# Attention: merging the two halves of a head's output by one wide copy, a transfer and a GpSimd add

## The chip, the cores and the metric

The kernel runs on one core of a Trainium2 chip. The metric is the device time of one execution in microseconds (us); the median of three runs of the kernel before is 1149.34 us (1149.09 to 1151.95).

## The reference

The program computes an attention layer with a learned position bias, then a dense layer with three gated products, then a mixture of eight experts. Only the attention part is touched here:

```python
scores = scale * np.matmul(q, k.transpose(0, 1, 3, 2))      # B, H, S, D = 2, 8, 576, 64
scores = scores + bias.transpose(2, 0, 1)[None, :, :, :]
scores = scores - np.max(scores, axis=-1, keepdims=True)
attn = np.exp(scores)
attn = attn / (np.sum(attn, axis=-1, keepdims=True) + 1e-09)
return np.matmul(attn, v).astype(np.float32)
```

Behind it come the two expert layers, which read the attention output of all heads.

## The kernel before, in words

**Precision.** Operands of the large products are split into a high part (a rounded copy) and a low part (the value less its high part). For the values V of a head this is the job of `prep_head` (L171): GpSimd copies V into the columns `hi` of a tile `vs` (the copy goes through the helper at L66), then subtracts to make the columns `lo` (L195). The two sets of 64 columns lie side by side, so one matmul with `vs` as weights gives both products at once: 64 PSUM partitions hold the product with the high parts and 64 the product with the low parts. `pv_ev` (L546) adds these halves.

**The steps.** The attention stage is one loop over steps `s`, nine to a head; below, `k` is the step within a head and a unit `u` is a block of 128 query rows of one batch element. In step `s` the program issues, for different units, the scores (`u_qk`, TensorE, L413), the maximum with the bias (`u_max`, VectorE, L430, writes `ng`), the exponential (`u_exp`, ScalarE, L441, reads `ng`, writes `pe`), transposes of `pe` on TensorE (L492, L501), and the split of the transposed block (ScalarE makes the high part at L505, VectorE the low part at L506). The products with V of head h run at the steps of head h+1 (L543). Their results leave PSUM in `pv_ev` at k = 3, 6 and 8 of head h+1, called below the first, second and third copy: 512 columns, then 320 and 320. ScalarE copies 64 partitions of PSUM to a tile `pvt` on the other 64 partitions (L554), and VectorE adds the other half of PSUM to it and writes `x32` (L556).

**GpSimd's order.** GpSimd makes the parts of the next head: Q of batch element 0 and 1 at k = 0 and 1, K at k = 2 and 3, V at k = 6 and 8. In the odd heads 3, 5 and 7 it also runs `x_out` (L563): three passes over 576 columns for each batch element, at k = 2 and k = 4, which normalise the two finished heads and split the result. Head 7 has no next head to prepare.

**Buffers.** Tiles of the pool `up` have two buffers unless the line says otherwise: `pvt` two, `ng` three, `r` (the reciprocals of a pair of heads) one. A new tile waits until all that reads the old one in its buffer is done. The PSUM tile `pv` has one buffer.

**The SP queue.** All transfers of this stage are issued from SP in program order: the bias tile of four tiles ahead at even k, the next inputs at k = 1, and at k = 4 the reciprocals: `r_d` is written to DRAM, and two transfers `r<-r_d` bring it back, which wait for that write. A transfer that waits holds up all that stand behind it.

Of the kernel before, what the change touches and what calls it, by code (L numbers as in the profile page):

```python
# [10 lines left out]
F32 = mybir.dt.float32  # L11
# [4 lines left out]
AF = mybir.ActivationFunctionType  # L16
ALU = mybir.AluOpType
# [4 lines left out]
B, H, S, D = 2, 8, 576, 64  # L22
# [29 lines left out]
def raw(ap):  # L52
    return ap.bitcast(F32)


def make_body(stop=None):
    def body(tc, a):
        nc = tc.nc
        ctx = ExitStack()
        V, A, G, T = nc.vector, nc.scalar, nc.gpsimd, nc.tensor  # L60

        def dma(out, in_):
            nc.sync.dma_start(out=out, in_=in_)

        def pool_copy(out, in_, scale=1.0):
            G.tensor_scalar(out=out, in0=in_, scalar1=scale, scalar2=1.0, op0=ALU.mult, op1=ALU.mult)  # L66
# [4 lines left out]
        def pool(name, bufs=1, space=None, side=None):  # L71
            kw = {}
            if space is not None:
                kw["space"] = space
            if side is not None:
                kw["side"] = side
            return tc.tile_pool(name=name, bufs=bufs, **kw)

        with ctx, tc.manual_schedule():
# [91 lines left out]
            def prep_head(h, k, part=None):  # L171

                p = h % 2
                qk, vr = raw_t[h]
                if k in (0, 2):
                    b = k // 2
                    hi = qs[p][b][:, 64 * b:64 * b + S]
                    lo, src = hi[64:128], qk[:, b, 0]
                    rest, hr = src[64:128], lo
                else:  # L180
                    if k in (4, 6):
                        b = k // 2 - 2
                        hi, lo, src = kh[p][b], kl[p][b], qk[:, b, 1]
                    else:
                        b = k - 7
                        oh = 64 * (h % 2)
                        ol = 64 - oh
                        hi, lo, src = vs[p][b][:, :, oh:oh + D], vs[p][b][:, :, ol:ol + D], vr[:, b]
                    rest, hr = src, hi
                if part in (None, 0):  # L190
                    pool_copy(hi, src)
                n = lo.shape[1]
                m = (n + 1) // 2
                for sl in {None: (slice(0, n),), 0: (), 1: (slice(0, m),), 2: (slice(m, n),)}[part]:
                    G.tensor_tensor(out=lo[:, sl], in0=rest[:, sl], in1=raw(hr[:, sl]), op=ALU.subtract)  # L195
# [12 lines left out]
            with ExitStack() as bctx:  # L208
# [80 lines left out]
                for q in range(2):  # L289
                    V.tensor_tensor(  # L290
                        out=wf[:, q, :].rearrange("p (i h) -> p i h", h=H),
                        in0=ab[:, q, :].unsqueeze(1).to_broadcast([128, 4, H]),
                        in1=msk.rearrange("p (i h) -> p i h", h=H), op=ALU.mult)
# [45 lines left out]
                v3 = lambda x: x.rearrange("p (f n) -> p f n", f=3)  # L339
# [14 lines left out]
                for g16 in range(NG16):  # L354
                    ps = bias_mm(g16)
# [31 lines left out]
            with ExitStack() as actx:  # L387
                pt_p = actx.enter_context(pool("pt"))
                up = actx.enter_context(pool("up", bufs=2))
# [6 lines left out]
                CW = (256, 320)  # L396
# [25 lines left out]
                def u_max(u):  # L422
                    h, k = divmod(u, 9)
                    w = un[u]
                    ng = up.tile([128, S], F32, tag="ng", name="ng", bufs=3)
                    if k == 0:

                        st_t[h] = up.tile([128, 2, 9], F32, tag="st", name="st", bufs=3)
                    c = U_COL[k]
                    V.tensor_tensor_reduce(  # L430
                        out=ng.rearrange("p (f n) -> p f n", f=2), in0=w["sc"][:, :, :SH],
                        in1=bias_t[h, k // 2].rearrange("p (f n) -> p f n", f=2),
                        op0=ALU.add, op1=ALU.min, scale=-0.125, scalar=3.0e38, accum_out=st_t[h][:, 0, c:c + 1])
                    w["ng"] = ng
# [94 lines left out]

                x32 = [None]  # L530
                pvs = {}

                def pv_mm(h, ch, bs, i0, i1):
                    if i0 == 0:
# [11 lines left out]
                def pv_ev(h, ch, bs):  # L546
                    ps = pvs.pop((h, ch, bs))
                    om = 64 * (h % 2)
                    oc = 64 - om
                    if h % 2 == 0 and ch == 0:  # L550
                        x32[0] = up.tile([128, 2, S], F32, tag="x32", name="x32")
                    n = len(bs) * CW[ch]
                    tmp = up.tile([128, 512], F32, tag="pvt", name="pvt")
                    A.activation(out=tmp[om:om + 64, :n], in_=ps[oc:oc + 64, :n], func=AF.Copy)  # L554
                    v3 = lambda x: x.rearrange("p (b i) -> p b i", b=len(bs))
                    V.tensor_tensor(out=x32[0][om:om + 64, bs[0]:bs[-1] + 1, 256 * ch:256 * ch + CW[ch]],  # L556
                                    in0=v3(ps[om:om + 64, :n]), in1=v3(tmp[om:om + 64, :n]), op=ALU.add)
                    if h % 2 == 1 and ch == 0:
                        x_t[h] = x32[0], r_t[0]

# [26 lines left out]
                def m1_first(n):  # L587

                    for _ in range(n):
# [9 lines left out]
                PV = {0: (9, 0, (0, 1), 0, 6), 1: (10, 0, (0, 1), 6, 12), 2: (11, 0, (0, 1), 12, 18),  # L599
                      4: (13, 1, (0,), 0, 5), 5: (14, 1, (0,), 5, 9), 7: (16, 1, (1,), 0, 9)}  # L600
                EV = {3: (12, 0, (0, 1)), 6: (15, 1, (0,)), 8: (17, 1, (1,))}
                PREP = {0: 0, 1: 2, 2: 4, 3: 6, 6: 7, 8: 8}
                LAGL = (5, 4, 3, 3, 4, 3, 3, 3, 4)
                R = {2: (11, r_add, r_inv), 3: (12, r_tr), 4: (13, r_out)}

                def at(f, u):
                    if 0 <= u < NU:
                        return f(u)

                for s in range(NU + 18):  # L610
                    h, k = divmod(s, 9)
                    at(u_qk, s)
                    if s == 1:
                        pv = ps_v.tile([128, 512], F32, tag="pv", name="pv")
                        for _ in range(NW2):
                            T.matmul(out=pv, lhsT=qs[0][0][:, 0:128], rhs=qs[0][0][:, 0:512], start=True, stop=True)
                    at(u_tr, s - 3)
                    for d in (5, 4, 3):
                        if s >= d and LAGL[(s - d) % 9] == d:
                            at(u_trl, s - d)  # L620
                    at(u_max, s - 1)
                    lo = at(u_ev, s - 4)
                    at(u_exp, s - 2)
                    if lo is not None:
                        lo()
                    if k in R and 0 <= (s - R[k][0]) // 9 < H:
                        for f in R[k][1:]:
                            f((s - R[k][0]) // 9)
                    if s < NU and k in PREP and h + 1 < H:
                        prep_head(h + 1, PREP[k])  # L630
                    for off, b in ((20, 0), (22, 1)):
                        if s > off and (s - off) % 18 == 9 and (s - off) // 9 < H - 1:
                            x_out((s - off) // 9, b)
                    if k in EV and 0 <= (s - EV[k][0]) // 9 < H:
                        pv_ev((s - EV[k][0]) // 9, *EV[k][1:])
                    for d, e in ((4, 3), (4, 7), (5, 8)):
                        lo = at(u_evl, s - d) if (s - d) % 9 == e else None
                        if lo is not None:
                            lo()
                    if k in PV and 0 <= (s - PV[k][0]) // 9 < H:  # L640
                        pv_mm((s - PV[k][0]) // 9, *PV[k][1:])
                    if k in W_AT and s < NU:
                        w_step(last=2)
                    elif s >= NU + 4:
                        w_step(2, last=3)
                    if s < NU:
                        if k % 2 == 0 and 5 * h + k // 2 + 4 < 5 * H:
                            load_bias(5 * h + k // 2 + 4)
                        if k == 1:
                            load_head(h + 2)  # L650
                    un.pop(s - 6, None)
                    if s == NU + 2:
                        for b in range(B):
                            x = x32[0][:64, b]
                            G.tensor_tensor(out=x, in0=x, in1=r_t[0][:64, b], op=ALU.mult)
                    if s == NU + 4:
                        r_mm()
                    m1_first(EARLY.get(s, 0))
                    if s - 9 * (H - 1) in (15, 17):
                        x_last((s - 9 * (H - 1) - 15) // 2)  # L660
# [18 lines left out]
            with ExitStack() as mctx:  # L679
# [8 lines left out]
                with pool("mp", bufs=2) as mp:  # L688
                    w_pool[:] = mp, 6
                    for f in range(6):  # L690
                        for g in range(NTG):
# [3 lines left out]
                            t2 = mp.tile([128, TG], F32, tag="t2", name="t2")  # L695
# [105 lines left out]
                for n, g in enumerate((0, 2, 1, 3)):  # L801
# [3 lines left out]
                    for d in range(4):  # L805
                        p = ps_o.tile([128, 512], F32, tag="o", name="o")
                        k = 0
# [294 lines left out]
```

## Time and profile before

| | us |
|---|---|
| median of three runs | 1149.34 |
| the profiled execution, its time | 1150.27 |
| the profiled execution, its span | 1148.5 |
| attention stage, from the first L430 to the last L578 | about 83 to 232 |

The profile shows one execution. Times in its rows are counted from the span's start. Engines are PE (TensorE; PEld its weight loads), DVE (VectorE), ACT (ScalarE), POOL (GpSimd); SPq is SP's queue of transfers. Over the whole span PE is busy 97%, DVE 62%, ACT 44% and POOL 33%.

### The profile page before, as it was taken

Reading aid. Unit: us, or ns where it says so; the run is one execution under the profiler, and the core shown is the slowest. Engines: PE = TensorE matmul, PEld = TensorE weight load, DVE = VectorE, ACT = ScalarE, POOL = GpSimd, SP = SyncE. Lnnn points to the kernel's source line nnn. Section 1 sums busy time; section 2 is a strip of 40 time slices with the busy share of each in tenths; the row PEclk is TensorE's granted clock in tenths of the full one; section 3 lists DMA queues with packets and bytes.
Section 4 is the critical chain, followed back from the end, with each engine's and each line's share of the span. In section 5 each row is a group of like instructions: output and inputs, shape, how many; then the busy total and the mean of one; then the engine's idle time right before and its main releaser. Section 6 shows DMA issues by size and latency. Waiting matters only on the chain.

```text
span 1148.5 us, 18982 instructions
## 1 busy us (share of the span) xinstructions
PE 1115.9 (97%) x7578; PEld 999.8 (87%) x7578; DVE 711.9 (62%) x1241; ACT 506.7 (44%) x879; POOL 373.3 (33%) x307
## 2 busy tenths in 40 slices
PE   6989999999999999999999999999999999999998
PEld 3448889999999899898998989989899898998986
DVE  7999999787752766554645636446365463554633
ACT  5988988633333553341522505325143151341520
POOL 3996789222212613220311202113022131220310
PEclk8999999999999999999999999999999999999999
DMA  3666665123310210210201102112021120210102
GB/s 140 229 230 216 210 187 166 41 92 110 111 42 14 93 37 13 62 47 28 74 26 49 49 27 74 37 38 70 14 65 40 34 74 10 64 47 28 56 19 82
DMA packets 35286, 87.45 MB, mean 76 GB/s; under 512 B 5439, under 2 KB 5630, under 8 KB 34302
## 3 DMA queue, kind: packets, MB, share of 16 engines
q1 hardware_dynamic: 35054, 85.96, 23.5%
q8 instruction: 59, 0.97, 0.3%
q10 hardware_dynamic: 144, 0.29, 0.1%
q14 instruction: 29, 0.24, 0.1%
HBM read 73.23 MB, written 13.01 MB: 75 GB/s over the span
## 4 chain that ended last, share of the span: by engine, by line
PE 70%; DVE 16%; issue 4%; ACT 2%; DMA 1%; DVEq 0%; ACTq 0%; SPq 0%
PE d L1014 34%; PE x L932 11%; PE y L932 8%; PE z L932 8%; PE o L810 3%; DVE ng L430 3%; DVE ptl L506 3%; PE m L584 2%; DVE ww L105 1%; DVE ww L108 1%; DVE ww L110 1%; DVE pth L506 1%; DVE x L556 1%; DMA wf<-in_moe_w 1%; ACT ww L104 1%
## 5 line engine op out<-in xcount | busy, mean ns | idle before, releaser
L1025 DVE SCALAR_TENSOR_TENSOR acc<-d,P,acc 128x512 f32<-128x512 f32 x135 | 101.3, 750 | 240.1 <-PE d L1014 240.0
L1000 POOL TENSOR_TENSOR w2l<-w2r,w2h 128x512 fp32r<-128x512 f32 x64 | 94.0, 1470 | 465.3 <-ACT w2h L999 457.0
L1014 PE MATMUL d<-w2h,hh 128*128 128x512 f32 x576 | 225.0, 391 | 0.0
L1014 PE MATMUL d<-w2h,hl 128*128 128x512 f32 x576 | 224.7, 390 | 0.0
L1014 PE MATMUL d<-w2l,hh 128*128 128x512 f32 x576 | 224.3, 389 | 0.0
L940 ACT ACTIVATE s<-x 128x576 f32<-128x576 f32 x96 | 62.5, 651 | 355.3 <-PE x L932 352.1
L945 ACT ACTIVATE hh<-s 128x576 fp32r<-128x576 f32 x128 | 87.9, 687 | 95.6 <-DVE s L957 46.3
L1014 PEld LDWEIGHTS d<-w2h,hl 128*128 128x128 f32 x576 | 108.1, 188 | 23.1 <-DVE hl L950 0.3
L1014 PEld LDWEIGHTS d<-w2l,hh 128*128 128x128 f32 x576 | 108.2, 188 | 22.1
L1014 PEld LDWEIGHTS d<-w2h,hh 128*128 128x128 f32 x576 | 108.2, 188 | 21.8
L950 DVE SCALAR_TENSOR_TENSOR hl<-s,hh 128x576 fp32r<-128x576 f32 x128 | 103.4, 826 | 1.7 <-ACT hh L945 1.5
L750 POOL TENSOR_TENSOR w1l<-wf,w1h 128x768 fp32r<-128x768 f32 x32 | 59.3, 1853 | 76.6 <-ACT w1h L749 76.6
L932 PE MATMUL x<-xth,w1h 128*128 128x288 f32 x384 | 82.6, 297 | 0.5 <-ACT acc L813 0.5
L932 PE MATMUL x<-xtl,w1h 128*128 128x288 f32 x384 | 82.2, 296 | 0.0
L932 PE MATMUL x<-xth,w1l 128*128 128x288 f32 x384 | 82.1, 295 | 0.0
L584 PE MATMUL m<-xh,wh 128*128 128x384 f32 x216 | 74.1, 343 | 1.8 <-DVE t L702 1.8
L333 PE MATMUL p<-s,wb 128*32 128x192 f16 (+1 forms) x1152 | 60.9, 295 | 13.1 <-DVE s L307 8.0
L584 PE MATMUL m<-xl,wh 128*128 128x384 f32 x216 | 73.6, 341 | 0.0
L584 PE MATMUL m<-xh,wl 128*128 128x384 f32 x216 | 73.5, 340 | 0.0
L333 PEld LDWEIGHTS <-wb 128*32 128x32 f16 x1152 | 31.8, 97 | 42.4 <-issue 31.1
L966 DVE TENSOR_TENSOR s<-y,s 128x576 f32<-128x576 f32 x32 | 24.2, 758 | 70.8 <-ACT w1h L753 58.9
L932 PEld LDWEIGHTS x<-xth,w1h 128*128 128x128 f32 x384 | 62.5, 188 | 2.0 <-ACT acc L813 0.7
(186 smaller groups left out, 2547.1 us busy)
## 6 DMA issues: line engine op xcount, KB each, us to landing
wf<-in_moe_w SPq DMA_DIRECT2D x32, 512.0 KB, 3.5
w2r<-in_moe_w SPq DMA_DIRECT2D x64, 256.0 KB, 2.6
bias_d<-bo SPq DMA_DIRECT2D x36, 288.0 KB, 2.7
bias<-bias_d SPq DMA_DIRECT2D x32, 288.0 KB, 3.6
wr<-in_moe_w SPq DMA_DIRECT2D x18, 512.0 KB, 3.7
qk<-in_qk SPq DMA_DIRECT2D x7, 1152.0 KB, 6.9
wr<-in_moe_w_out SPq DMA_DIRECT2D x6, 512.0 KB, 3.6
vr<-in_v SPq DMA_DIRECT2D x8, 320.0 KB, 4.3
```

What stands on the lines that cost most here:

```text
L333: T.matmul(out=thirds(pt)[32 * c:32 * c + 32, sl, :], lhsT=wb[p][:, q, :], rhs=s_t[4 * g16 + c][:, sl, :], start=(p == 0), stop=(p == 1))
L430: V.tensor_tensor_reduce(out=ng.rearrange("p (f n) -> p f n", f=2), in0=w["sc"][:, :, :SH], in1=bias_t[h, k // 2].rearrange("p (f n) -> p ...
L506: return lambda: V.tensor_tensor(out=lo, in0=src, in1=raw(hi), op=ALU.subtract)
L584: T.matmul(out=p[:, :TG], lhsT=ws[:, 128 * c:128 * c + 128], rhs=xs[:, c, TG * g:TG * g + TG], start=(c == 0 and n == 0), stop=(c == 3 and ...
L750: G.tensor_tensor(out=lo[:, 0:3], in0=t[:, 1:4], in1=raw(hi[:, 0:3]), op=ALU.subtract)
L932: T.matmul(out=ps[bank][:, s, :SH], lhsT=ws[:, i, c, :], rhs=xs[:, j, c, s * SH:s * SH + SH], start=(start and k == 0), stop=(k == 5), **kw)
L940: A.activation(out=t, in_=src, func=AF.Copy)
L945: A.activation(out=o, in_=src, func=AF.Relu)
L950: V.scalar_tensor_tensor(out=l, in0=src, scalar=0.0, in1=raw(o), op0=ALU.max, op1=ALU.subtract)
L1000: G.tensor_tensor(out=lo, in0=r, in1=raw(hi), op=ALU.subtract)
L1014: T.matmul(out=pd, lhsT=hs[:, fh, 128 * t:128 * t + 128], rhs=ws, start=(k == 0), stop=(k == 11))
L1025: V.scalar_tensor_tensor(out=acc[:, t, :], in0=pd, scalar=P[:, t, e:e + 1], in1=acc[:, t, :], op0=ALU.mult, op1=ALU.add)
```

## The change

- The high part of V for the next head (k = 6 and 8) is a copy on ScalarE and no longer on GpSimd. The low part stays on GpSimd.
- `pv_ev` for heads 0 to 6: ScalarE copies all 128 partitions of PSUM into `pvt`; a transfer from the SP queue moves the 64 partitions of the other half into a new tile `pv2` with one buffer; GpSimd adds the two halves into `x32`. The add is put off: it is issued two steps after the copy, that is at k = 5, 8 and 1 (of the next head), before `x_out` of the same step and behind `prep_head`. Head 7 keeps the old way.
- `ng` has two buffers in place of three.

```diff
-                if part in (None, 0):
+                if part is None and k > 6:
+                    A.activation(out=hi, in_=src, func=AF.Copy)
+                elif part in (None, 0):
                     pool_copy(hi, src)
...
-                    ng = up.tile([128, S], F32, tag="ng", name="ng", bufs=3)
+                    ng = up.tile([128, S], F32, tag="ng", name="ng", bufs=2)
...
+                adds = []
...
                     tmp = up.tile([128, 512], F32, tag="pvt", name="pvt")
-                    A.activation(out=tmp[om:om + 64, :n], in_=ps[oc:oc + 64, :n], func=AF.Copy)
...
+                    if h < H - 1:
+
+                        t2 = up.tile([128, 512], F32, tag="pv2", name="pv2", bufs=1)
+                        A.activation(out=tmp[:, :n], in_=ps[:, :n], func=AF.Copy)
+                        dma(t2[om:om + 64, :n], tmp[oc:oc + 64, :n])
+                        adds.append((9 * h + PV_AT[ch, bs] + 2, lambda: G.tensor_tensor(
+                            out=out, in0=v3(tmp[om:om + 64, :n]), in1=v3(t2[om:om + 64, :n]), op=ALU.add)))
+                    else:
+                        A.activation(out=tmp[om:om + 64, :n], in_=ps[oc:oc + 64, :n], func=AF.Copy)
+                        V.tensor_tensor(out=out, in0=v3(ps[om:om + 64, :n]), in1=v3(tmp[om:om + 64, :n]), op=ALU.add)
...
+                PV_AT = {e[1:]: e[0] for e in EV.values()}
...
+                    while adds and adds[0][0] <= s:
+                        adds.pop(0)[1]()
```

## Rows read from the trace of the kernel before

**Rows 1.** Windows by head, third copy to third copy: length, then busy time per engine

```profile
core 0: us, PE busy (x) PEld busy (x) DVE busy (x) ACT busy (x) POOL busy (x), PEclk, DMA share, GB/s
110.35:127.39 17.04, 16.54 (x127) 15.42 (x125) 16.67 (x37) 15.33 (x36) 11.58 (x13) 1.00 0.53 177
127.39:143.98 16.59, 16.02 (x125) 15.15 (x124) 16.30 (x36) 15.31 (x35) 15.83 (x15) 1.00 0.70 230
143.98:161.61 17.63, 16.05 (x120) 14.48 (x119) 17.31 (x37) 15.22 (x34) 14.52 (x17) 1.00 0.62 200
161.61:178.74 17.13, 16.32 (x124) 15.03 (x123) 16.84 (x38) 14.96 (x35) 16.24 (x15) 1.00 0.56 180
178.74:195.45 16.71, 16.55 (x129) 15.67 (x128) 16.33 (x37) 15.05 (x35) 15.39 (x18) 1.00 0.51 130
195.45:211.42 15.97, 15.83 (x125) 15.19 (x124) 15.69 (x36) 14.56 (x34) 9.26 (x8) 1.00 0.39 122
110.35:211.42 101.07, 97.32 (x737) 90.95 (x736) 99.15 (x216) 90.43 (x207) 82.82 (x83) 1.00 0.55 174
```

**Rows 2.** Chain that ended last, 110.35 to 211.42 us, shares by line

```profile
by line: DVE ng L430 29.0%; DVE ptl L506 24.9%; issue 11.4%; DVE pth L506 8.6%; DVE x L556 7.2%; PE sc L413 4.5%; PE pv L543 3.6%; DVE st L448 3.2%; PE pt L492 2.4%; DVE st L430 1.5%; DVE ww L106 0.7%; DVE ww L110 0.7%; DVE ww L108 0.7%; AC
```

**Rows 3.** Groups by form, 110.35 to 211.42 us: count, busy us, mean ns, idle before

```profile
L556 DVE TENSOR_TENSOR x<-pv,pvt 64x320 f32<-64x320 f32 x12 | 5.8, 484 | 0.2
L556 DVE TENSOR_TENSOR x<-pv,pvt 64x512 f32<-64x512 f32 x6 | 4.1, 684 | 0.1
...
L554 ACT ACTIVATE pvt<-pv 64x320 f32<-64x320 f32 x12 | 5.2, 433 | 0.3
L554 ACT ACTIVATE pvt<-pv 64x512 f32<-64x512 f32 x6 | 3.6, 592 | 0.1
L505 ACT ACTIVATE pth<-pt 128x512 fp32r<-128x512 f32 x54 | 32.1, 595 | 8.7 <-PE pt L492 7.7
...
L66 POOL TENSOR_SCALAR vs<-vr 128x320 fp32r<-128x320 f32 x11 | 5.4, 492 | 9.6 <-PE pv L543 9.6
L195 POOL TENSOR_TENSOR vs<-vr,vs 128x320 fp32r<-128x320 f32 x11 | 9.9, 903 | 0.9
L113 POOL TENSOR_TENSOR wl<-ww,wh 128x512 fp32r<-128x512 f32 x2 | 2.6, 1291 | 0.1
L568 POOL TENSOR_TENSOR x<-x,r 128x576 f32<-128x576 f32 x6 | 8.6, 1431 | 0.0
```

**Rows 4.** Timeline, ACT at 182 and DVE at 183 us: an exponential, the next-but-one maximum

```profile
182.43 0.77 ACT L441 ACTIVATE pe<-ng,st 128x576 f32<-128x576 f32 x1
...
183.19 0.74 DVE L430 CUSTOM_DVE_ANT_0 ng<-sc,bias 128x576 f32<-128x576 f32 x1
```

**Rows 5.** Timeline of POOL: the stretches up to the end of x_out, heads 3 and 5

```profile
128.23 0.68 POOL L66 TENSOR_SCALAR qs<-qk 128x576 fp32r<-128x576 f32 x1
...
145.63 0.46 POOL L66 TENSOR_SCALAR vs<-vr 128x320 fp32r<-128x320 f32 x1
...
162.94 0.68 POOL L66 TENSOR_SCALAR qs<-qk 128x576 fp32r<-128x576 f32 x1
...
180.17 0.46 POOL L66 TENSOR_SCALAR vs<-vr 128x320 fp32r<-128x320 f32 x1
```

**Rows 6.** Timeline of ACT: the third copy of head 3

```profile
143.98 0.43 ACT L554 ACTIVATE pvt<-pv 64x320 f32<-64x320 f32 x1
```

**Rows 7.** Timeline of SP's queue: the reciprocals of two heads coming back

```profile
125.97 1.26 SPq L63 DMA_DIRECT2D r<-r_d  x2
...
159.22 1.26 SPq L63 DMA_DIRECT2D r<-r_d  x2
```

**Rows 8.** DMA issues, 96 to 212 us: KB each, median us to landing

```profile
bias<-bias_d SPq DMA_DIRECT2D x14, 144.0 KB, 3.0
```

**Rows 9.** Windows as in rows 1, where the granted clock was low

```profile
224.00:226.00 2.00, 2.00 (x8) 2.00 (x8) 1.28 (x3) 0.53 (x2) 0.00 (x0) 0.50 0.00 0
226.00:228.00 2.00, 2.00 (x12) 2.00 (x11) 1.20 (x3) 1.22 (x2) 1.29 (x1) 0.79 0.51 152
```

More of the change, by code (lines that the diff above doesn't have):

```diff
@@ L553, in pv_ev @@
                     tmp = up.tile([128, 512], F32, tag="pvt", name="pvt")
-                    A.activation(out=tmp[om:om + 64, :n], in_=ps[oc:oc + 64, :n], func=AF.Copy)
                     v3 = lambda x: x.rearrange("p (b i) -> p b i", b=len(bs))
-                    V.tensor_tensor(out=x32[0][om:om + 64, bs[0]:bs[-1] + 1, 256 * ch:256 * ch + CW[ch]],
-                                    in0=v3(ps[om:om + 64, :n]), in1=v3(tmp[om:om + 64, :n]), op=ALU.add)
+                    out = x32[0][om:om + 64, bs[0]:bs[-1] + 1, 256 * ch:256 * ch + CW[ch]]
+                    if h < H - 1:
[7 more added lines that the diff above has]
+                        V.tensor_tensor(out=out, in0=v3(ps[om:om + 64, :n]), in1=v3(tmp[om:om + 64, :n]), op=ALU.add)
                     if h % 2 == 1 and ch == 0:
```

## The prediction

> **What bounds the kernel now.** I looked first at the windows by head, because the change touches the attention stage alone and the shares of the whole span say nothing of it. From the third copy of head 1 at 110.35 us to that of head 7 at 211.42 us six heads take 101.07 us; DVE is busy 99.15 of them, 98%, PE 97.32, ACT 90.43 and POOL 82.82 [rows 1]. The reader should see that one engine is full and that the other three are not far behind. Then the chain that ended last: it runs along DVE's maximum, its low parts and the adds of L556, which alone hold 7.2% [rows 2]. So DVE sets the pace, and work taken off DVE can shorten a head, until the next engine is full. Third, the waits beside the groups: POOL idles 9.6 us for PE ahead of the copies of V [rows 3]. That looks like room for adds, but it must be seen head by head: POOL is busy 15.83 of 16.59 us and 16.24 of 17.13 us in the stretches that hold the x_out passes of heads 3 and 5, and 9.26 of 15.97 us in the last [rows 1]. Its room is where head 7 prepares nothing and where no x_out runs.
>
> **Part 1: DVE is relieved.** Per head one add of 0.684 and two of 0.484 us go [rows 3], 1.65 us; DVE's 99.15 / 6 = 16.5 us become 14.9. ACT gains two copies of V of 320 columns; the nearest row is the copy of 64x320, 0.433 us [rows 3], so 0.87 us: 90.43 / 6 = 15.07 becomes 15.9 us. The PSUM copy over 128 partitions instead of 64 costs nothing more: 128x512 took 595 ns and 64x512 592 ns [rows 3]. At k = 6 and 8 the new copies wait for the same matmuls as the PSUM copy right behind them, so they add no wait. PE's weight loads are busy 90.95 / 6 = 15.2 us [rows 1]. An undisturbed head would then take 16.1 us, just above ACT's sum; at best 15.2 (PE), at worst 16.4. Against rows 1 this saves 0.9 us in the stretch 110.35:127.39, 1.5 in 143.98:161.61, 0.6 in 178.74:195.45, nothing in 195.45:211.42, and I give 0.5 to head 1, where two of the three adds fall before its third copy. **Saving 3.5 us**; with 15.2 us a head 1.8 + 2.4 + 1.5 + 0.8 and 1.0 for head 1, 7.5; with 16.4 us 0.6 + 1.2 + 0.3 + 0.2, 2.3. The stretches of heads 3 and 5 are not in this sum: part 3 has them.
>
> **Part 2: two buffers for ng.** A maximum then waits for the exponential of two units before. In the tightest place I found that exponential ends at 182.43 + 0.77 = 183.20 us and the maximum starts at 183.19 [rows 4]; elsewhere there is more. I take 0: with DVE relieved and PE feeding it, DVE has no reason to be earlier. Cover gone, 0.5 us in all.
>
> **Part 3: POOL is late in heads 3 and 5, and ACT has to wait for it.** This decides. pvt has two buffers, so the third copy (k = 8) takes the buffer of the first copy (k = 3) and must wait until the add of that one has been made on POOL. That add is issued at k = 5, behind everything POOL has before it: Q and K of the next head, the add of the previous head's third copy, and both x_out passes. Before the change DVE freed that buffer within the step.
>
> The prices: an add of 512 columns between 1.29 us (two inputs, 512 columns, L113) and 1.43 us (576, L568); an add of 320 columns 0.90 us (L195) [rows 3]. I take 1.36 and 0.89.
>
> Head 3: POOL starts it at 128.23 us and works without a gap until both x_out passes are done at 145.63, 17.40 us [rows 5]. Now two adds stand in between, 2.25 us: 19.65. The start moves too. At the least the add of head 2's second copy comes in at k = 8 and one copy of V goes (0.89 us less 0.49 and its spacing, 0.35 us). At the most that add waits for its transfer, which sits in SP's queue behind the reciprocals that are issued at 125.97 for 1.26 us [rows 7]: one more bias issue of some 0.35 us, then 3.0 us for a transfer of 144 KB, the nearest in size to 80 KB [rows 8], so landing near 130.6, add done 131.5. The add of the first copy ends between 128.58 + 19.65 = 148.2 and 131.5 + 19.65 = 151.15 us. The third copy of head 3 ran at 143.98 [rows 6]. The stretch grows by 4.2 to 7.2 us; I take 5.5. In those clocks all parts shift alike by what heads 1 and 2 gain, so this holds whatever they gain.
>
> The Trainium skill ("DMA: Bandwidth & Descriptors", the section on fixed cost) puts some 2.0 us fixed on a transfer plus its bytes at 436 GB/s. By that an 80 KB transfer would be an estimated 2.2 us and the upper end 0.8 us lower; 80 KB within the core was not measured here.
>
> Head 5: POOL works from 162.94 to 180.17, 17.23 us [rows 5], and with two adds 19.5. Start at the least 0.35 later, at the most behind the reciprocals at 159.22 [rows 7]: 159.22 + 1.26 + 0.35 + 3.0 + 0.89 = 164.7. The add ends at 182.8 to 184.2, against a third copy at 178.74 [rows 1]: 4.1 to 5.5 us, I take 4.7. Head 7's third copy is safe, since POOL prepares nothing there.
>
> What stands behind ACT's wait: the high part of the next transposed block, without which DVE cannot make its low part, and the exponentials, without which PE has nothing to transpose. There are two score buffers and two ng buffers, so PE and DVE run ahead by about a step and then stand too; I let them win back 0.5 us after each wait (0 to 1). **Cost 5.5 + 4.7 - 1.0 = 9.2 us**, between 6.3 and 12.7.
>
> SP: three issues more per head, about 0.35 us each, and the transfer waits for ACT's copy and for pv2, which the previous add frees. Behind it stand the bias loads; they are issued four tiles ahead and while ACT waits nobody asks for them. I cost this at nothing; if that cover goes it is a late bias of 1 to 2 us in head 6.
>
> **The sum.** 9.2 - 3.5 = +5.7 us on the profiled execution: 1150.27 + 5.7 = 1156.0. Its time lies 0.93 us above the median of the runs, so on that scale 1149.34 + 5.7 = **1155.0 us**. The ends of the terms: 6.3 - 7.5 = -1.2 and 12.7 + 0.5 - 2.3 = +10.9, so 1148 to 1160.
>
> **The rivals.**
> *A, POOL keeps up and the relief of DVE counts in every head.* For it: 9.6 us of POOL's idle time [rows 3], and the adds are put off by two steps. Against: that idle time is not in front of the late adds. Heads 3 and 5 would also go to 16.1 us: 3.5 + 0.5 + 1.0 = 5.0 us saved, 1144.3. It decides if the add at k = 5 ends before the third copy in heads 3 and 5, that is if POOL's stretch there is under about 16 us. Chance 0.13.
> *B, the wait is there but costs about what is saved.* The wait at its low end, 8.3 less 2.0 won back, against savings of 6 to 7: within 1 us of 1149.3. Chance 0.17.
> *C, the pauses also cost clock.* At 224 to 226 us the granted clock was 0.50, the 1.2 GHz level, and 0.79 in the next 2 us, after a row of small matmuls [rows 9]: at 0.50 two us are worth one, so 1.0 + 0.4 = 1.4 us lost there. If PE standing for 4 us twice brought that each time, 2.8 us more: 1157.8. The Trainium skill ("TensorE: Matmul & The Clock Gate", Part 1) says an idle array falls back to 1.2 GHz; no row of this stage has such a pause, so no trace here shows it. Chance 0.20.
> The forecast itself 0.50.
>
> **How the numbers follow.** About 0.3%, 3.4 us, is what can be told from no change. The forecast and C lie above +3.4 us, with a tail of the forecast below: slower 0.68, same 0.19, faster 0.13. The range takes the upper end of the sum with C, cut at 1161, and reaches below into B, 1147.5; it leaves out A and the top of C.
>
> **What would show it.** Right: in the waits, ACT at the copy of heads 3 and 5 standing 4 to 7 us for POOL; third copies of heads 3 and 5 some 21 to 22 us after those of heads 2 and 4; other heads near 16.1; no L556 before head 7; POOL without idle time in heads 3 and 5. Wrong: no ACT wait on POOL over 2 us (then A), undisturbed heads still near 17 (then part 1 is too large), a granted clock under 1.00 between 140 and 200 us (then C).

## The result

The changed kernel takes 1161.43 us in the median of four runs (1159.2 to 1164.12), the kernel before 1149.68 beside it: a ratio of 1.0101, with a 95% interval of 1.0088 to 1.0115. It is slower, and by 11.8 us where 5.7 were forecast. The profiled execution took 1162.18 us with a span of 1160.4, 11.9 more than the span before, and that is what the profile has to account for.

The windows by head of the changed kernel, from third copy to third copy as in [rows 1] (columns as there):

```profile
109.30:126.66 17.36, 16.98 (x137) 16.54 (x136) 16.39 (x37) 15.42 (x39) 12.16 (x12) 1.00 0.63 196
126.66:152.95 26.29, 17.32 (x128) 15.35 (x125) 14.29 (x34) 15.17 (x37) 21.11 (x21) 0.95 0.54 172
152.95:168.92 15.97, 15.48 (x109) 15.09 (x110) 13.79 (x32) 14.62 (x37) 13.25 (x14) 0.88 0.64 203
168.92:192.18 23.26, 17.49 (x138) 16.59 (x136) 16.46 (x39) 14.79 (x38) 20.25 (x20) 0.98 0.55 168
192.18:208.62 16.44, 15.95 (x109) 15.88 (x110) 13.53 (x30) 15.09 (x37) 15.04 (x15) 0.83 0.52 138
208.62:225.17 16.55, 16.53 (x134) 16.02 (x132) 15.29 (x37) 14.18 (x35) 10.94 (x11) 1.00 0.41 127
109.30:225.17 115.87, 99.75 (x746) 95.47 (x744) 89.74 (x202) 89.27 (x218) 92.75 (x89) 0.94 0.55 168
```

The six stretches take 115.87 us instead of 101.07. DVE is busy 89.74 us instead of 99.15, so the relief is there; but no engine is full any more, and the time is idle time. Two stretches hold the loss, those that end at the third copies of heads 3 and 5: 26.29 instead of 16.59 and 23.26 instead of 17.13, together 15.83 us more.

The chain through the same time, against [rows 2]: DVE's maximum and its adds are gone from the front, and POOL, the new transfer and PE stand there.

```profile
by line: PE pv L546 10.7%; DMA pv<-pvt 10.6%; PE sc L415 9.3%; POOL x L564 8.8%; POOL x L579 7.3%; PE pt L494 7.2%; issue 6.9%; POOL xl L581 6.2%; POOL qs L197 4.9%; POOL kl L197 4.1%; ACT pe L443 3.7%; POOL xh L66 3.5%; DVE ptl L508 2.7%; 
```

The longest waits from 90 to 235 us (who waited for whom: us in total, times, longest). The copy out of PSUM is L562 now, the add L564, the maximum L432:

```profile
DVE ptl L508 <- ACT pth L507: 23.5, 13, 8.8
ACT pvt L562 <- POOL x L564: 21.5, 6, 9.1
...
PE pv L546 <- ACT pvt L562: 15.9, 4, 8.2
POOL x L564 <- DMA pv<-pvt: 14.3, 7, 4.3
```

Read from the bottom: POOL waits for the transfer, ACT for POOL's add, PE and DVE for ACT. The longest ACT waits are the third copies of heads 3 and 5; ACT's timeline shows them:

```profile
126.66 0.44 ACT L562 ACTIVATE pvt<-pv 128x320 f32<-128x320 f32 x1 [1.08 <-POOL x L564]
...
152.95 0.44 ACT L562 ACTIVATE pvt<-pv 128x320 f32<-128x320 f32 x1 [9.07 <-POOL x L564]
...
192.18 0.44 ACT L562 ACTIVATE pvt<-pv 128x320 f32<-128x320 f32 x1 [7.65 <-POOL x L564]
```

POOL's timeline around them, to be read beside [rows 5]: the adds of head 2's first and second copy, POOL's first work for head 3, the add of head 3's first copy; then, from the add of the second copy on, the same for heads 4 and 5.

```profile
125.34 1.28 POOL L564 TENSOR_TENSOR x<-pvt,pv 64x512 f32<-64x512 f32 x1 [2.60 <-ACT pe L443]
...
132.63 0.86 POOL L564 TENSOR_TENSOR x<-pvt,pv 64x320 f32<-64x320 f32 x1 [4.21 <-PE pt L494]
133.58 0.67 POOL L66 TENSOR_SCALAR qs<-qk 128x576 fp32r<-128x576 f32 x1
...
151.67 1.25 POOL L564 TENSOR_TENSOR x<-pvt,pv 64x512 f32<-64x512 f32 x1
...
172.63 0.88 POOL L564 TENSOR_TENSOR x<-pvt,pv 64x320 f32<-64x320 f32 x1 [2.07 <-PE pl L503]
173.60 0.68 POOL L66 TENSOR_SCALAR qs<-qk 128x576 fp32r<-128x576 f32 x1
...
190.89 1.25 POOL L564 TENSOR_TENSOR x<-pvt,pv 64x512 f32<-64x512 f32 x1
```

POOL starts head 3 at 133.58 us, 6.92 after the third copy of head 2; before it was 128.23, 0.84 after. From there it works 151.67 + 1.25 - 133.58 = 19.34 us to the end of the add of the first copy, and the third copy starts 0.03 us later. POOL starts head 5 4.68 us after the third copy of head 4 (1.33 before), and its work there takes 18.54 us. The profile names PE as what released the late adds; an add reads nothing of PE's, and what it needs besides ACT's copy is the transfer. SP's queue shows that transfer (it is named pv<-pvt):

```profile
119.36 0.50 SPq L63 DMA_DIRECT2D r_d<-rt  x1
124.86 1.26 SPq L63 DMA_DIRECT2D r<-r_d  x2
126.22 0.54 SPq L63 DMA_DIRECT2D bias<-bias_d  x1
126.93 0.49 SPq L63 DMA_DIRECT2D pv<-pvt  x1
...
133.52 0.49 SPq L63 DMA_DIRECT2D pv<-pvt  x1
```

The second copy was made at 121.83 us. Its transfer stands behind the reciprocals, which wait until 124.86 for their own write, and goes out at 126.93. The reciprocals were not all that held it: pv2's one buffer was in use until the add of the first copy was done, at 125.34 + 1.28 = 126.62. The transfer then lands 5.6 us after its issue, and the add starts 5.7 us after it. The third copy's transfer waits for pv2's buffer in turn, until 133.52.

Last, the granted clock around the first pause and behind the second (windows, columns as in [rows 9]), and two scores matmuls on PE's timeline at either level:

```profile
148.00:150.00 2.00, 0.00 (x0) 0.00 (x0) 0.00 (x0) 0.00 (x0) 1.91 (x3) 1.00 0.00 0
150.00:152.00 2.00, 0.00 (x0) 0.00 (x0) 0.00 (x0) 0.00 (x0) 1.92 (x3) 0.52 0.43 126
152.00:154.00 2.00, 0.56 (x2) 0.56 (x3) 0.09 (x1) 1.05 (x3) 2.00 (x3) 0.50 0.62 169
...
192.00:196.00 4.00, 3.33 (x16) 3.28 (x16) 2.50 (x5) 3.44 (x8) 3.44 (x6) 0.50 0.58 163
```
```profile
154.89 0.44 PE L415 MATMUL sc<-kh,qs 128*128 128x288 f32 x1
155.13 0.44 PE L415 MATMUL sc<-kl,qs 128*128 128x288 f32 x1
...
157.62 0.29 PE L415 MATMUL sc<-kh,qs 128*128 128x288 f32 x1
157.76 0.29 PE L415 MATMUL sc<-kl,qs 128*128 128x288 f32 x1
```

While PE, DVE and ACT all stand and only POOL works, the granted clock falls to 0.50, the 1.2 GHz level, and PE restarts at 0.24 us a matmul instead of 0.14. The stretch after each long pause has a mean clock of 0.88 and 0.83. "TensorE: Matmul & The Clock Gate" of the Trainium skill (Part 1) says that an idle array falls back to 1.2 GHz; in these two pauses the trace agrees.

### The profile page after: what moved, and what is told of

Its sections match the earlier page's. It is cut to its first block, busy times and chain, and to the rows that moved or that the text cites. A ratio compares the mean times of both kernels' runs of the same rounds, so it can differ in the third digit from the quotient of the medians.

```text
span 1160.4 us, 19007 instructions
## 1 busy us (share of the span) xinstructions
PE 1115.7 (96%) x7578; PEld 999.7 (86%) x7578; DVE 700.8 (60%) x1220; ACT 506.6 (44%) x893; POOL 384.7 (33%) x314
## 4 chain that ended last, share of the span: by engine, by line
PE 71%; DVE 8%; POOL 4%; ACT 3%; issue 3%; DMA 2%; SPq 0%; POOLq 0%; DVEq 0%; ACTq 0%
PE d L1028 34%; PE x L946 12%; PE y L946 8%; PE z L946 8%; PE o L824 3%; PE m L595 2%; PE sc L415 1%; PE pv L546 1%; DMA pv<-pvt 1%; DVE ww L105 1%; DVE ww L110 1%; DVE ww L108 1%; POOL x L564 1%; PE pt L494 1%; POOL x L579 1%
```

## The experiments

The theory after the result: POOL is late in heads 3 and 5, by the length of its own work and by transfers that come late, and ACT pays because pvt has two buffers. The rivals put the loss down to one of the parts: the buffers, the transfers, POOL's work, SP's order, or the two small edits. Each ratio is to the kernel before on the same chip, with its 95% interval. Four runs pay for a buffer with the fifth buffer of pe; a run with four buffers of pe and nothing else was not made, but in the waits of these four no exponential waits for a buffer of pe.

**Three buffers for pvt.** The space comes from pe, four buffers instead of five.

```diff
-                    pe = up.tile([128, S], F32, tag="pe", name="pe", bufs=5)
+                    pe = up.tile([128, S], F32, tag="pe", name="pe", bufs=4)
...
-                    tmp = up.tile([128, 512], F32, tag="pvt", name="pvt")
+                    tmp = up.tile([128, 512], F32, tag="pvt", name="pvt", bufs=3)
```

> The changed kernel with three buffers for pvt (paid for by four instead of five for pe). Theory (ACT's waits for the add on POOL, through the two buffers of pvt, make the loss): the third copies of heads 3 and 5, which waited 9.1 and 7.7 us, wait under 1 us; these heads go from 26.3 and 23.3 us to 16.5 to 17.5, the granted clock stays at 1.00, and the time falls by 12 to 15 us to 1146 to 1149. Rival (POOL has too much work in heads 3 and 5, and any buffer only moves the wait on): ACT's wait goes, but PE or SP waits for POOL instead, heads 3 and 5 stay above 20 us, and the time falls by less than 6 us, to 1156 or more.

Measured: 1157.99 us, ratio 1.0062 (1.0045 to 1.0079). The theory as I had put it fell. The rival held in the time and in the waits, but not in the heads it named: head 3 takes 17.3 us, and the loss moves on to heads 4, 5 and 6 with 21.7, 22.1 and 20.5 us. The wait at the third copies is gone; the waits from 143 to 200 us show where it went:

```profile
ACT pth L507 <- PE pt L494: 10.7, 10, 4.5
DVE ng L432 <- DMA bias<-bias_d: 7.7, 5, 2.3
...
POOL x L564 <- DMA pv<-pvt: 6.2, 4, 3.5
...
PEld sc L415 <- POOL kh L66: 2.6, 1, 2.6
PEld sc L415 <- POOL kl L197: 2.5, 3, 1.3
```

PE waits for K of the next head and DVE for a bias that is late: the reciprocals in front of it in SP's queue wait for their own write and for the passes of x_out that read their one buffer, which POOL makes late. The buffer of pvt is where POOL's lateness is felt first, and not the only place.

**No transfer.** The copied half is added to itself, so the other half is left out of the sum.

```diff
-                        t2 = up.tile([128, 512], F32, tag="pv2", name="pv2", bufs=1)
...
-                        dma(t2[om:om + 64, :n], tmp[oc:oc + 64, :n])
...
-                            out=out, in0=v3(tmp[om:om + 64, :n]), in1=v3(t2[om:om + 64, :n]), op=ALU.add)))
+                            out=out, in0=v3(tmp[om:om + 64, :n]), in1=v3(tmp[om:om + 64, :n]), op=ALU.add)))
```

> The changed kernel without the transfers: GpSimd adds the copied half to itself, so the other half is left out of the sum. Theory (POOL starts heads 3 and 5 late because the transfer of the second copy lands late, behind the reciprocals in SP's queue, and adds to a wait that is there anyway): POOL's first instruction for head 3 comes at most 2 us after the third copy of head 2 instead of 6.9, that of head 5 at most 2 instead of 4.7; ACT's waits fall from 9.1 and 7.7 to 3 to 5 us each; the time falls by 7 to 10 us to 1151 to 1154. Rival (the length of the adds alone): the waits fall by less than 1.5 us each and the time by less than 4 us.

Measured: 1153.21 us, ratio 1.0022 (1.0013 to 1.0032), 8.2 us below the changed kernel. POOL starts heads 3 and 5 1.94 us after the third copy in both, and ACT still waits, as its timeline shows:

```profile
148.26 0.44 ACT L561 ACTIVATE pvt<-pv 128x320 f32<-128x320 f32 x1 [5.19 <-POOL x L562]
...
185.12 0.44 ACT L561 ACTIVATE pvt<-pv 128x320 f32<-128x320 f32 x1 [2.85 <-POOL x L562]
```

Both waits lie a little outside the 3 to 5 us expected. So the late transfers are the larger part of the loss, and a wait remains without them. The 8.2 us are an upper bound for them, since these adds, which read one tile twice, are also shorter: 0.72 us for 320 columns against 0.87.

**The V copies alone** (the first edit of the diff on the kernel before).

> The kernel before with the high part of V on ScalarE and nothing else changed. Theory (ACT has room while DVE sets the pace): within 1 us of the kernel before, 1149 to 1150.5. Rival (the copies hold up ACT's exponentials at k = 6 and 8): 2 to 6 us slower, 1152 to 1156.

Measured: 1150.01 us, ratio 0.9998 (0.9989 to 1.0008). By themselves they cost and bring nothing that is clear of the noise.

**Two buffers for ng alone** (the second edit on the kernel before).

> The kernel before with two buffers for ng and nothing else changed. Theory (the exponential is done by the time the maximum two units later starts): 0 to 0.5 us slower, 1149.5 to 1150.2. Rival (DVE, which sets the pace, now waits for ACT every few units): 3 us slower or more, 1152.5 and up.

Measured: 1150.24 us, ratio 0.9994 (0.9985 to 1.0004). Nothing clear of the noise either.

**The reciprocals later.** The two transfers r<-r_d move out of `r_out` into a function of their own, three steps later.

```diff
+                def r_back(h):
...
-                R = {2: (11, r_add, r_inv), 3: (12, r_tr), 4: (13, r_out)}
+                R = {2: (11, r_add, r_inv), 3: (12, r_tr), 4: (13, r_out), 7: (16, r_back)}
```

> The changed kernel with the reciprocals' two transfers issued at k = 7 instead of k = 4, so that the transfer of the second copy (k = 6) no longer stands behind them in SP's queue. Theory (that place in the queue makes POOL start heads 3 and 5 late): the transfer of head 2's second copy is issued within 2 us of its copy instead of 5.1, POOL's first instruction for head 3 comes at most 3 us after the third copy of head 2 instead of 6.9; ACT's waits at the third copies of heads 3 and 5 fall to 5 to 7 and 3.5 to 5.5 us; the time falls to 1153.5 to 1157. Rival (the transfers are late by themselves, by their own landing time and by pv2's one buffer): POOL still starts head 3 over 4.5 us after the third copy, and the time stays above 1158.5.

Measured: 1155.71 us, ratio 1.0056 (1.0040 to 1.0072), 5.7 us below the changed kernel. ACT waits 6.89 and 5.20 us, and POOL starts head 3 3.06 us after the third copy, a hair outside what was expected. One expectation missed: the second copy's transfer goes out 4.3 us after its copy and not within 2, because it now waits for pv2, whose add waits for its own transfer. The rows show the transfer, its add, and then the stretches of heads 3, 5 and 6 (windows, columns as in [rows 1]):

```profile
127.55 0.48 SPq L63 DMA_DIRECT2D pv<-pvt  x1
...
129.65 0.87 POOL L568 TENSOR_TENSOR x<-pvt,pv 64x320 f32<-64x320 f32 x1 [0.33 <-DMA pv<-pvt]
...
127.55:150.06 22.51, 16.76 (x132) 15.86 (x130) 15.47 (x34) 15.29 (x37) 21.20 (x21) 0.99 0.58 183
...
166.79:188.23 21.44, 18.07 (x142) 17.12 (x140) 17.29 (x39) 14.99 (x38) 20.20 (x20) 1.00 0.55 168
188.23:203.45 15.22, 14.13 (x109) 13.51 (x110) 13.05 (x30) 14.89 (x37) 14.15 (x14) 1.00 0.63 173
```

The transfer goes out together with the third copy (127.55), hardly sooner than in the changed kernel (0.27 us after it). What changed in head 3 is the time from its issue to its add: 2.1 us, where it was 5.7 with the reciprocals issued just ahead of it. In head 5 both changed: it goes out 0.77 us before the third copy instead of 0.46 after, and the add follows 2.1 us later instead of 3.25. Why a transfer lands later behind the reciprocals, no run shows.

**Two buffers for pv2** (four for pe).

```diff
-name="pv2", bufs=1)
+name="pv2", bufs=2)
```

> The changed kernel with two buffers for pv2 (paid for by four instead of five for pe) and nothing else. Theory (pv2's one buffer and the place behind the reciprocals each make the transfers late; the place is the larger part): the transfer of head 2's second copy still goes behind the reciprocals, that of the third copy no longer waits for an add; POOL starts head 3 4 to 6.5 us after the third copy of head 2; the time is 1157 to 1161. Rival (pv2's buffer is the whole delay): POOL starts head 3 at most 3 us after the third copy, time 1153 to 1156.

Measured: 1157.64 us, ratio 1.0065 (1.0047 to 1.0082). POOL starts head 3 4.4 us after the third copy. The buffer brings 3.8 us, the place in the queue 5.7.

**Both.**

> The changed kernel with two buffers for pv2 (four for pe) and the reciprocals' transfers at k = 7: both causes of the late start are gone, the two buffers of pvt stay. Theory (what is left is the length of POOL's own work before the add of the first copy, 19.5 us against some 16 to the third copy): POOL starts heads 3 and 5 at most 3 us after the third copy before them, ACT waits 4.5 to 6.5 us in head 3 and 3.5 to 5.5 in head 5, time 1152.5 to 1156. Rival (the waits were made by the late transfers): ACT's waits under 2.5 us each, time under 1150.

Measured: 1155.29 us, ratio 1.0041 (1.0026 to 1.0056), 6.1 us below the changed kernel and not clear of the run with the later reciprocals alone: the two gains do not add up. POOL starts heads 3 and 5 2.8 and 2.1 us after the third copy, and ACT still waits:

```profile
150.66 0.44 ACT L566 ACTIVATE pvt<-pv 128x320 f32<-128x320 f32 x1 [6.90 <-POOL x L568]
...
187.50 0.44 ACT L566 ACTIVATE pvt<-pv 128x320 f32<-128x320 f32 x1 [5.20 <-POOL x L568]
```

The first wait is 0.4 us over what I expected, the second inside. With more punctual transfers the change still loses 4.7 us on the kernel before (1155.29 less 1150.6): this is what the longer work of POOL costs and the relief of DVE does not pay back, with whatever the clock adds.

**Three buffers for pvt and the reciprocals later.**

> The changed kernel for all heads, with three buffers for pvt (four for pe) and the reciprocals' transfers at k = 7: neither the buffer nor the place in the queue holds anybody up. Theory (POOL's own work, about 21 us in heads 3 and 5 and 13.7 in heads 2, 4 and 6, is then the bound, 17.4 us a head over a pair): heads 3 and 5 above 17.5 us and the time at 1150 to 1154. Rival (the two waits were all): heads 3 and 5 at 16.5 us, time 1145 to 1148.

Measured: 1151.41 us, ratio 1.0014 (1.0004 to 1.0025). No copy waits over 0.8 us for an add now. The stretches that end at the third copies of heads 5 and 6 (windows, columns as in [rows 1]):

```profile
160.11:179.90 19.79, 16.49 (x125) 15.18 (x125) 16.43 (x35) 15.11 (x37) 15.00 (x15) 1.00 0.71 221
179.90:199.36 19.46, 17.23 (x127) 15.47 (x126) 14.51 (x32) 15.55 (x38) 18.19 (x19) 1.00 0.44 121
```

Head 3 is not held up (16.30 us), against what I expected; heads 5 and 6 pay, 19.79 and 19.46 us. That POOL's work is the bound is not shown: it is busy 18.19 us of the second stretch, but only 15.00 of the first, where it stands 3.8 us for a transfer, that of a copy made at 150.21 us, which waited for pv2's one buffer until 158.57 and landed 7.9 us later, while DVE waits 2.9 us for a bias. So late transfers still have a part in it.

**Only heads 1, 3 and 5 the new way**, so that no first or second copy of an x_out head goes over POOL.

```diff
-                    if h < H - 1:
+                    if h % 2 and h < H - 1:
```

> The changed kernel with the new way only for heads 1, 3 and 5, whose copies fall in steps of the even heads 2, 4 and 6, where POOL runs no x_out; all other heads keep the copy of 64 partitions and the add on VectorE. Theory (the loss is in heads 3 and 5 alone, the relief of DVE pays elsewhere): no wait of ACT for POOL over 1 us, heads 2, 4 and 6 at 16.0 to 16.6 us, heads 3 and 5 at 16.5 to 17.5, time 1146 to 1149.5. Rival (POOL still starts the odd heads 5 us or more late, and bias or K come late): heads 3 and 5 above 18 us, time 1151 to 1155.

Measured: 1152.03 us, ratio 1.0022 (1.0011 to 1.0033): the rival, though in another head than it said. Heads 3 and 5 take 16.28 and 17.43 us, but head 4 takes 21.0: POOL starts head 3 5.2 us after the third copy, with the transfer still behind the reciprocals; x_out then frees the reciprocals' one buffer late, SP sends them at 148.49 us instead of 143.42, and from 143 to 165 us DVE waits 2.0 us for a bias and PE 1.7 for K.

**The same with the reciprocals later.**

> Both: the new way only for heads 1, 3 and 5, and the reciprocals' transfers at k = 7. Theory: as in the run with heads 1, 3 and 5 alone, and POOL starts heads 3 and 5 at most 3 us after the third copy before them; time 1145.5 to 1148.5. Rival (DVE is not relieved where it matters, or ACT's copies of V cost as much): within 1 us of the kernel before, 1149.5 to 1151.5.

Measured: 1146.93 us, ratio 0.9974 (0.9964 to 0.9983). This beats both kernels. Its windows by head:

```profile
111.22:127.88 16.66, 16.17 (x127) 15.40 (x126) 15.73 (x37) 15.53 (x38) 10.88 (x11) 1.00 0.65 206
127.88:144.16 16.28, 16.09 (x126) 15.37 (x125) 15.37 (x37) 15.75 (x38) 15.19 (x16) 1.00 0.75 245
144.16:161.58 17.42, 16.82 (x133) 16.10 (x132) 16.73 (x38) 15.19 (x37) 16.43 (x15) 1.00 0.65 197
161.58:178.11 16.53, 14.72 (x109) 13.20 (x108) 15.35 (x32) 15.59 (x37) 15.38 (x15) 1.00 0.67 210
178.11:194.00 15.89, 15.89 (x129) 15.69 (x129) 14.96 (x36) 15.23 (x38) 15.10 (x15) 1.00 0.56 154
194.00:209.00 15.00, 15.00 (x121) 14.65 (x120) 14.39 (x33) 14.45 (x35) 11.74 (x11) 1.00 0.43 111
```

97.78 us in place of 101.07, 3.3 less, with a clock of 1.00 in every head. POOL is at work 16.43 of 17.42 us in the fullest stretch, and one copy there still waits 1.24 us for it. Where the gain comes from is not shown: 1.4 us of it fall in heads 2, 4 and 6, whose adds left DVE, and 1.9 in heads 3, 5 and 7, which keep theirs. The three small edits together (V on ScalarE, two buffers for ng, reciprocals later) without any add moved were not run.

**The control: the reciprocals later, on the kernel before.**

> The kernel before with the reciprocals' two transfers at k = 7 and nothing else changed: the control for the run that was faster than both kernels. Theory (that run gained by the relief of DVE; the transfers' place matters only to the new transfers): within 0.8 us of the kernel before, 1149 to 1150.7. Rival (the gain came from the place in the queue): 2 to 3.5 us faster than the kernel before.

Measured: 1149.53 us, ratio 0.9994 (0.9985 to 1.0003). That is 1.1 us below the kernel before beside it, a little more than expected but not clear of the noise. So the faster run did not gain by the queue's order alone.

**All heads but 2, 4 and 7 the new way, reciprocals later.**

```diff
-                    if h < H - 1:
+                    if h not in (2, 4) and h < H - 1:
```

> The new way for all heads but 2, 4 and 7, with the reciprocals' transfers at k = 7: heads 0 and 6, whose copies fall in steps of heads 1 and 7, are added to heads 1, 3 and 5; only the copies in steps of heads 3 and 5 stay the old way. Theory (every head in which POOL has room gains by DVE's relief): head 1 and head 7 each 0.3 to 0.8 us shorter than with heads 1, 3 and 5 alone, time 1145.5 to 1147. Rival (these heads are held by PE and ACT by now): the same as with heads 1, 3 and 5, 1146.5 to 1148.

Measured: 1147.43 us, ratio 0.9973 (0.9962 to 0.9983), the same as with heads 1, 3 and 5. The rival held: heads 0 and 6 bring nothing more that could be told.

## Why the prediction was right and wrong

**Right: the sign, the place and the mechanism.** ACT stands at the third copies of heads 3 and 5 for POOL's add of the first, with DVE and PE behind it.

**Right: the length of POOL's work.** 19.34 and 18.54 us against 19.65 and 19.5; the adds took 0.87 and 1.27 us against 0.89 and 1.36. With the reciprocals later and nothing else changed the loss is 5.8 us (1155.71 less 1149.87), where 5.7 were forecast, and there the terms fit too: heads 3 and 5 take 10.2 us more than before (forecast 10.2), the stretches of heads 2, 4, 6 and 7 together 4.6 less (forecast 3.0, and 1.0 won back). The sum I made was that of a kernel whose transfers land sooner. That the totals agree to 0.1 us is luck: that profile also holds 1.2 us lost up to the third copy of head 1 and 2.3 gained after that of head 7, which no term forecast.

**Wrong: when POOL starts.** The step that failed is "then 3.0 us for a transfer of 144 KB, the nearest in size to 80 KB, so landing near 130.6, add done 131.5", which I had called the most. The transfer was issued when the sum said, 0.27 us after the third copy of head 2 (the sum: 127.58 against 127.39), but it landed 5.6 us later and not 3.0. Landing took 2.6 us in the median for 80 KB and 4.6 for 128 KB, and from 2.0 to 5.6 over those 12 of the 21 transfers whose landing the profile tells:

```profile
pv<-pvt SPq DMA_DIRECT2D x14, 80.0 KB, 2.6
...
pv<-pvt SPq DMA_DIRECT2D x7, 128.0 KB, 4.6
```

A median of another transfer is no upper bound. "DMA: Bandwidth & Descriptors" of the Trainium skill (the section on the anatomy of one DMA, whose fit is for transfers issued from GpSimd) led to an estimate of 2.2 us for 80 KB; issued from SP, the quick ones here took 2.0 and the late one 5.6. The start came 6.92 and 4.68 us after the third copies, where the sum allowed 4.1 and 3.1 at most, and the values I took, 5.5 and 4.7 us of growth, stand for about 2.4 each. In head 3 the landing is 2.6 of the 2.8 us above the most. In head 5 it was 3.1 us, as assumed; there the reciprocals went out 0.8 us later against the third copy than before, and the bias and the transfer behind them 0.5 later than costed. Starts later by 4.5 and 2.3 us than taken, with work shorter by 0.3 and 1.0, make 10.2 + 6.8 - 1.3 = 15.7 us, where the two stretches grew by 15.83. Of the changed kernel's 11.8 us some 5.7 go with the place of the reciprocals in SP's queue, which is what moving them takes away. I had seen that order, and still cost SP "at nothing"; the issues, too, took 0.49 us each and not 0.35.

**Wrong: only two waits.** Four other copies waited too: 1.08 us for the third of head 2, 0.99 and 1.06 for the first and second of head 3, 1.63 for the third of head 7, which I had called safe: POOL prepares nothing there, but the add of the first copy stands behind both x_out passes and ends at 225.14. That makes 4.8 us of the 21.5 us of ACT's wait. Head 2 saves nothing, where 0.9 us were forecast, and head 7 takes 0.58 us more; that these waits are the reason is likely but not tested.

**Part 1, too large.** 3.5 us were forecast outside heads 3 and 5. Measured: -0.32, 1.66, 0.27 and -0.58 in heads 2, 4, 6 and 7, together 1.0, and 1.05 up to the third copy of head 1 (at 109.30 instead of 110.35). That last part need not be the relief: the control, which is the kernel before with the reciprocals later, makes this copy at 109.14 us with every add still on DVE. "An undisturbed head 16.1 us" is not tested here: heads 4 (15.97) and 6 (16.44) begin with a low clock, and what PE and DVE did ahead during the wait counts in them too. Nor does a single profile tell such sizes well: with two buffers for ng alone, head 5 is 1.2 us longer than before at the same total.

**Part 2 and the copies of V.** Nothing clear of the noise, as forecast, each shown alone.

**The account.** +15.83 in the stretches of heads 3 and 5 (forecast +9.2), -2.1 in the others (forecast -3.5), and -1.85 after the last third copy, which was not forecast: together +11.9. In that tail the low clock of [rows 9] is gone, the granted clock is 1.00 from 222 to 244 us; I had put 1.4 us on it there. The other runs do not bear out that this is the gain: with two buffers for ng alone the low clock is there, and the tail is 935.3 us against 935.2 in the changed kernel and 937.1 in the kernel before. Its cause stays open.

**The rivals.** A and B fell. C came true beside the forecast: PE, back at work at 153.44 and 192.67 us, ran at 0.50 until 156.9 and 197.9, 3.5 and 5.2 us, of which half is lost on PE: 1.7 and 2.6. How much of it reaches the end stays open, but the limit is 4.3 us. One comparison says that it is less: in three runs ACT's wait in head 5 is 5.2 us and PE stands 3.4 us in it. With the reciprocals later the clock stays at 1.00; with two buffers for pv2, and with both, it is at 0.50 when PE works again. The stretch behind the wait takes 15.22 us in the first and 15.59 and 15.64 in the others, 0.4 us more. The 5.7 us that the queue's order makes are not explained by the clock.

## What to carry to other kernels

Before work is moved to an engine with room on average, lay its new list out in program order in the fullest stretch, and find which buffer's release hangs on the last item: there another engine will wait. A transfer put into an in-order queue takes over every wait that stands ahead of it (the reciprocals went out 5.5 us after their write), it landed later right behind them (5.6 us against 2.1 or less), and its landing time needs a spread, not a median. A move that fails when it is made in every head can pay where the target engine has room: here, for the three heads whose copies fall in heads where POOL runs no x_out, with the two small edits and the queue put in order, it is worth 0.26%.

## What the runs showed of the hardware that was not expected

Transfers of one kind inside the core landed after 2.0 to 5.6 us, median 3.3, in the changed kernel, and one of 128 KB after 7.9 us in the run with three buffers for pvt and the reciprocals later. The granted clock fell to 0.50 while PE stood from 145.3 to 153.4 us, and it stayed there for the first 3.5 us of work. Around a pause of 3.4 us it fell to 0.50 in two runs and stayed at 1.00 in a third. GpSimd's add of 64x320 took 0.72 us where both operands were the same tile and 0.87 where they were two.
